# Two chunks' columns by transposing transfers, row factors by element transfers, and a reordered transfer queue in a mixer kernel

## The chip, the cores and the metric

The kernel runs on one core of a Trainium2 chip. The metric is the device time of one execution in microseconds (us), the median of several runs. Engines: PE (TensorE, matrix products and transposes), DVE (VectorE), ACT (ScalarE), POOL (GpSimd), and SP (SyncE), which here only issues transfers.

## The reference

```python
x = A_x                                  # (1, 2048, 512), bf16
xn = _layernorm(x, axis=-1)
s = _A_ref(xn, A_wqkv, A_wo)             # 32 heads of 16, 8 keys at distance 2, softmax, then @ wo
g = _silu(_B_ref(xn, B_w1, B_w2, B_w3, B_w4))
return x + s * g

def _B_ref(x, w1, w2, w3, w4):           # D = 512, F = 1376
    h = _gelu(_layernorm(x, axis=-1) @ w1)
    ...                                  # four groups of columns of h, shifted by 1, 1, 2, 2 rows: g0 to g3
    hs = jnp.concatenate([g0, g1, g2, g3], axis=-1) @ w2
    x1 = x + hs
    return x1 + _gelu(_layernorm(x1, axis=-1) @ w3) @ w4
```

The layer norm in `_B_ref` is applied to rows that are already normalised. It comes down to one more factor per row.

## The kernel before, in words

The 2048 rows are split into even rows (p = 0) and odd rows (p = 1), 1024 each, and each half into two chunks of 512 rows (`CH`): chunks 0 and 1 are even rows, 2 and 3 odd. A chunk is four tiles of 128 rows (`TPC`). `xn[p]` holds rows, with rows on the 128 partitions; `xnT[p]` holds the same numbers with columns on the partitions, which the products need.

For each chunk the front part of the kernel does the following.

- `Norm` (`stats` L221 and L223 on DVE, `root` L204 and L205 on POOL, `apply` L237 on DVE) normalises the rows in place.
- `turn` (L296) gets the columns: each call does eight PE transposes of 128x128 (L302), half a chunk, into a PSUM bank, and one DVE copy (L303) to `xnT`.
- `rows2` (L248) makes the second norm's row factors on POOL: 512 numbers as a 128x4 tile `r2b`.
- The factors have to stand along the free axis, the same on all partitions. `rows2_spread` (L264, chunks 1 and 2) does that by a PE transpose of the 128x4 tile (L266), a DVE copy (L268), a write of four rows of 256 bytes to DRAM (`r2_d`, L269) and a broadcast read of the 1 KB row to 128 partitions (L271). `rows2_here` (L273, chunks 0 and 3) does it on the chip: a diagonal on DVE (L277), one product with ones on PE (L282) and a copy out of PSUM (L284 on ACT, or L286 on DVE).
- `scaled` (L288) multiplies the columns by the factors on DVE (L291) into `xn2Ts[c]`.
- `q_all`, `k_all` and `v_pair` are the projections of mixer A; `w1` (L397) is mixer B's first product with its gelu. `v_pair` also writes its result to DRAM (`v_d`, L377, two transfers of 256 KB a call).

Then `w2` (L415) multiplies the shifted columns of h by w2 and adds the result to the rows; `columns` (L443) normalises, writes the chunk to DRAM (L446) and reads it back with a transposing transfer (L450); `w3` (L459) and the attention with `g_w4` follow.

Every instruction is pinned in program order on its engine, so each engine runs its list from top to bottom and the order in the listing (L501 to L599) is the order on each engine. The same holds for SP: a transfer whose data is not ready holds back all that stand behind it. Transfers use eight semaphores in turn, and a ninth waits for the first. PSUM results go through `pair()`: three pairs of banks in rotation.

The lines around the change: `rows2_spread(1)` at L544, the load of w3 at L545, `turn(2, ..)` at L566 and L567, `turn(3, ..)` at L571 and L572, the load of w4 at L574, `rows2_here(3)` at L579, `w1` of chunks 2 and 3 at L581 to L584, `w2(0)` at L585, `columns(0)` at L586, `w3(0)` at L592.

Of the kernel before, what the change touches and what calls it, by code (L numbers as in the profile page):

```python
# [8 lines left out]
AF = mybir.ActivationFunctionType  # L9
ALU = mybir.AluOpType  # L10
BF16 = mybir.dt.bfloat16
# [9 lines left out]
def kernel(  # L21
# [17 lines left out]
    PE, DVE, ACT, POOL, SP = nc.tensor, nc.vector, nc.scalar, nc.gpsimd, nc.sync  # L39

    def pin(ins):

        return tc.keep_in_program_order(ins)

    P = 128
    S = 2048
    D = 512
    F = 1376
    ND = D // P
# [4 lines left out]
    CH = 512  # L54
    NCH = S // CH
    TPC = CH // P
    M = S // 2
# [21 lines left out]
    dram = ctx.enter_context(tc.tile_pool(name="dram", bufs=1, space=bass.MemoryType.DRAM))  # L79
    psp = ctx.enter_context(tc.tile_pool(name="psp", bufs=1, space=bass.MemoryType.PSUM))  # L80

    def b8(shape, name):
        return big.tile(shape, BF16, name=name, tag="b8")

    def b4(shape, name):
        return sm4.tile(shape, BF16, name=name, tag="b4")
# [9 lines left out]
    def single():  # L96
        cnt["s"] += 1
        return PS[:, 6 + (cnt["s"] - 1) % 2, :]
# [27 lines left out]
    w3_sb = wpl.tile([P, WS], BF16, name="w3_sb", tag="w")[:, 0 : ND * F].rearrange("p (dt f) -> p dt f", f=F)  # L126
# [4 lines left out]
    ident = const.tile([P, P], BF16, name="ident")  # L131
# [61 lines left out]
    xnT = [b8([P, ND, M], f"xnT{p}") for p in range(2)]  # L193
# [2 lines left out]
    kM = [kbp.tile([P, ND, MK, 2], BF16, name=f"kM{p}", tag="kM") for p in range(2)]  # L196
    v_d = [dram.tile([MK, 2, D], BF16, name=f"v_d{p}") for p in range(2)]
    r2_d = dram.tile([NCH, CH], BF16, name="r2_d")
    x1n_dram = dram.tile([S, D], BF16, name="x1n_dram")
    vst = [b4([P, 2, 2, D], f"vst{i}") for i in range(2)]  # L200

# [5 lines left out]
    def small_t(name, shape, dt=F32):  # L207
        return small.tile(shape, dt, name=name, tag=name)
# [33 lines left out]
    def x_of(c):  # L242
        p, k = c // 2, c % 2
        return xn[p][:, k * TPC : (k + 1) * TPC, :]

    xn2Ts, r2s = {}, {}

    def rows2(c, ln):  # L248

        r2 = small_t("r2", [P, TPC])  # L250
        r2b = small_t("r2b", [P, TPC], BF16)
        eng = DVE if c == 0 else POOL
        pin(eng.tensor_tensor(out=r2, in0=ln.rstd, in1=ln.rstd, op=ALU.mult))
        pin(eng.tensor_tensor(out=r2, in0=r2, in1=ln.mv[:, :, 1], op=ALU.mult))
        if c == 0:
            pin(ACT.activation(r2, r2, AF.Sqrt, bias=eps_t[:]))
            with nc.allow_low_precision("bf16 row factors"):
                pin(DVE.reciprocal(out=r2b, in_=r2))
        else:
            rsqrt_eps(r2, r2)  # L260
            pin(POOL.tensor_copy(out=r2b, in_=r2))
        r2s[c] = r2b

    def rows2_spread(c):  # L264
        pt = single().bitcast(BF16)[0:TPC, 0:P]
        pin(PE.transpose(pt, r2s[c], ident[:]))  # L266
        t = small_t("r2t", [TPC, P], BF16)
        pin(DVE.tensor_copy(out=t, in_=pt))  # L268
        pin(SP.dma_start(out=r2_d[c].rearrange("(j q) -> j q", q=P), in_=t))  # L269
        xn2Ts[c] = b4([P, ND, CH], "xn2T")  # L270
        pin(SP.dma_start(out=xn2Ts[c][:, ND - 1, :], in_=r2_d[c : c + 1, :].to_broadcast([P, CH])))  # L271

    def rows2_here(c):  # L273

        xn2Ts[c] = t = b4([P, ND, CH], "xn2T")
        d = t[:, 0, :].rearrange("p (j q) -> p j q", q=P)
        pin(DVE.tensor_tensor(  # L277
            out=d, in0=ident.unsqueeze(1).to_broadcast([P, TPC, P]), in1=r2s[c].unsqueeze(2).to_broadcast([P, TPC, P]),
            op=ALU.mult,
        ))  # L280
        pt = single()
        pin(PE.matmul(pt, lhsT=ones_bf[:], rhs=t[:, 0, :], start=True, stop=True))  # L282
        if c == 0:
            pin(ACT.activation(t[:, ND - 1, :], pt, AF.Copy))  # L284
        else:
            pin(DVE.tensor_copy(out=t[:, ND - 1, :], in_=pt))  # L286

    def scaled(c):  # L288
        p, k = c // 2, c % 2
        t = xn2Ts[c]  # L290
        pin(DVE.tensor_tensor(  # L291
            out=t, in0=xnT[p][:, :, k * CH : (k + 1) * CH],
            in1=t[:, ND - 1, :].unsqueeze(1).to_broadcast([P, ND, CH]), op=ALU.mult,
        ))

    def turn(c, h):  # L296
        p, k = c // 2, c % 2
        i = k * TPC + 2 * h
        pt = single().bitcast(BF16).rearrange("p (a j q) -> p a j q", a=ND, j=2)
        for j in range(2):  # L300
            for dt in range(ND):
                pin(PE.transpose(pt[:, dt, j, :], xn[p][:, i + j, dt * P : (dt + 1) * P], ident[:]))  # L302
        pin(DVE.tensor_copy(  # L303
            out=xnT[p][:, :, i * P : (i + 2) * P], in_=pt.rearrange("p a j q -> p a (j q)")
        ))

    def turn_one(c, t):
        p, k = c // 2, c % 2
        i = k * TPC + t
        pt = single().bitcast(BF16)[:, 0 : ND * P].rearrange("p (a q) -> p a q", a=ND)  # L310
        for dt in range(ND):
            pin(PE.transpose(pt[:, dt, :], xn[p][:, i, dt * P : (dt + 1) * P], ident[:]))
        pin(ACT.activation(xnT[p][:, :, i * P : (i + 1) * P], pt, AF.Copy))

    def q_half(pts, lo, hi, nts=range(ND)):
        for nt in nts:
# [17 lines left out]
    def chunk(t, c):  # L334
        p, k = c // 2, c % 2
        return t[p][:, :, k * CH : (k + 1) * CH]
# [12 lines left out]
    def k_all(c, parts=(0, 1)):  # L349
        p, k = c // 2, c % 2  # L350
        for a in parts:
            pt = proj(c, a, wqk_sb[:, :, D : 2 * D], chunk(xnT, c))
            for e in range(2):
                pin(ACT.activation(  # L354
                    kM[p][:, 2 * a : 2 * a + 2, 8 + k * CH : 8 + (k + 1) * CH, e], pt, AF.Copy, scale=em[:, e : e + 1]
                ))
# [29 lines left out]
    def v_pair(p, t):  # L386
        pt = pair()
        for i in range(2):
            v_mm(p, t + i, pt[:, i, :])
        v_keep(p, t, 2, pt[:, 0, :])  # L390

    def v_pad(p):
        rows = v_d[p].rearrange("r e d -> (r e) d")
        pin(SP.dma_start(out=rows[0:16], in_=zero[0:16, :]))
        pin(SP.dma_start(out=rows[2 * (M + 8) : 2 * MK], in_=zero[0:4, :]))

    def w1(c, a):  # L397
        p, k = c // 2, c % 2
        pt = proj(c, a, w1_sb, xn2Ts[c])
        pin(ACT.activation(  # L400
            hT[p][:, 2 * a : 2 * a + 2, 1 + k * CH : 1 + (k + 1) * CH], pt, AF.Gelu_apprx_tanh
        ))
# [12 lines left out]
    def w2(c, order="a0 s0 a1 s1"):  # L415

        p, k = c // 2, c % 2
        x_c = x_of(c)
        ln = ln2[c] = Norm(x_c, b4([P, TPC, D], "xn3"), TPC, "l3")
        pts = []  # L420
        for h in range(TPC // 2):
            pt = pair()
            pts.append(pt)
            for j in range(2):
                m0 = k * CH + (2 * h + j) * P
                for g in range(ND):
                    pin(PE.matmul(  # L427
                        pt[:, j, :], lhsT=w2_src(p, g, m0), rhs=w2_sb[:, g, :],
                        start=(g == 0), stop=(g == ND - 1),
                    ))  # L430
        for what, i in (w for w in order.split()):
            if what == "a":
                h = int(i)
                xs = x_c[:, 2 * h : 2 * h + 2, :]
                pin(DVE.tensor_tensor(out=xs, in0=pts[h], in1=xs, op=ALU.add))  # L435
            elif what == "s":
                h = int(i)
                ln.stats(2 * h, 2 * h + 2)
            else:
                columns(c - 1)  # L440
        ln.root()
# [87 lines left out]
    for a in range(2):  # L529
# [10 lines left out]
    v_pair(0, 2)  # L540
    k_all(0, (1,))
    v_pad(0)
    w1(0, 0)
    rows2_spread(1)  # L544
    pin(SP.dma_start(out=w3_sb, in_=B_w3.rearrange("(dt q) f -> q dt f", q=P)))  # L545
    turn(1, 0)
    turn(1, 1)
    w1(0, 1)
    l2 = Norm(x_of(2), x_of(2), TPC, "l1")
    l2.stats(0, 4)  # L550
    l2.root()
    l2.apply(0, 4)
    rows2(2, l2)
    l3 = Norm(x_of(3), x_of(3), TPC, "l1")
    l3.stats(0, 4)
    l3.root()
    scaled(1)
    q_all(1)
    k_all(1)
    v_pair(0, 4)  # L560
    l3.apply(0, 4)
    rows2(3, l3)
    v_pair(0, 6)
    rows2_spread(2)
    w1(1, 0)
    turn(2, 0)  # L566
    turn(2, 1)  # L567
    w1(1, 1)
    scaled(2)
    q_all(2)  # L570
    turn(3, 0)  # L571
    turn(3, 1)  # L572
    k_all(2)
    pin(SP.dma_start(  # L574
        out=w4_sb[:, 0 : NF - 1, :],
        in_=B_w4[0 : (NF - 1) * P, :].rearrange("(ft q) n -> q ft n", q=P),
    ))
    pin(SP.dma_start(out=w4_sb[0:FL, NF - 1, :], in_=B_w4[(NF - 1) * P : F, :]))
    rows2_here(3)  # L579
    scaled(3)  # L580
    w1(2, 0)  # L581
    w1(2, 1)
    w1(3, 0)
    w1(3, 1)  # L584
    w2(0)  # L585
    columns(0)  # L586
    v_pad(1)
    q_all(3)
# [289 lines left out]
    for n in range(NU):  # L878
        now["n"] = n
        q = W4 * (n + 1) // NU - given  # L880
# [111 lines left out]
```

## Time and profile before

| what | value |
|---|---|
| time, median of three runs | 197.82 us (197.75 to 199.02) |
| the profiled execution | 197.26 us |
| its span in the trace | 195.5 us, so 1.76 us lie around it |
| granted TensorE clock | 0.996 |
| DVE, ACT, POOL busy | 60%, 68%, 10% of the span |
| transfers | 28.12 MB, mean 144 GB/s |

A time in a list is the start from the beginning of the span and then the duration, both in us; an arrow in brackets names what an engine's idle time ended with. SPq lines are transfers as SP issues them; the duration there is the time of issuing, not of moving the data.

### The profile page before, as it was taken

How to read it: one execution, taken by the hardware profiler on the slowest of the kernel's cores; microseconds unless marked ns; L12 is line 12 of the kernel's file. 1: busy time of each engine (PE TensorE's matmuls, PEld its weight loads, DVE VectorE, ACT ScalarE, POOL GpSimd, SP SyncE). 2: the span in 40 equal slices, each digit the busy share in tenths (PEclk: the TensorE clock that was granted, in tenths of full speed). 3: DMA queues.
4: the chain of work that ended last, by engine and by line, in shares of the span. 5: the costliest groups of instructions: out<-in, count | busy, mean ns of one | idle time of the engine just before them, and what ended most of it. 6: DMA issues, size and time to landing. Idle time of an engine off the chain costs nothing.

```text
span 195.5 us, 5255 instructions
## 1 busy us (share of the span) xinstructions
PE 185.5 (95%) x2253; PEld 91.8 (47%) x2283; DVE 117.8 (60%) x229; ACT 133.3 (68%) x151; POOL 19.1 (10%) x57
## 2 busy tenths in 40 slices
PE   7899999999999999999999999999999999999990
PEld 2474544554444444444444444445444544554540
DVE  5785767236076697494200035556487888798894
ACT  7399769649817615435656588877887876887871
POOL 3006066100002022006000000000000000000000
PEclk9999999999999999999999999999999999999998
DMA  4997480654000433752480051457565556582523
GB/s 131 339 368 239 132 282 15 218 158 157 0 0 3 136 83 109 215 107 65 110 260 0 0 162 60 157 166 232 153 216 161 137 155 215 127 247 51 171 91 126
DMA packets 33576, 28.12 MB, mean 144 GB/s; under 512 B 10760, under 2 KB 32528, under 8 KB 33552
## 3 DMA queue, kind: packets, MB, share of 16 engines
q1 hardware_dynamic: 33408, 27.71, 47.2%
q8 instruction: 18, 0.29, 0.6%
q10 hardware_dynamic: 144, 0.07, 0.1%
q14 instruction: 6, 0.05, 0.1%
HBM read 17.01 MB, written 8.67 MB: 131 GB/s over the span
## 4 chain that ended last, share of the span: by engine, by line
PE 85%; DMA 5%; DVE 4%; issue 2%; SPq 1%; ACT 1%
PE PS L469 19%; PE PS L328 19%; PE PS L764 19%; PE PS L427 5%; PE PS L811 4%; PE PS L795 4%; PE PS L652 3%; DMA wqk_sb<-in_A_wqkv_dram 3%; PE PS L626 3%; PE PS L362 3%; DMA x1nT<-x1n_dram 2%; PE PS L318 2%; PE PS L662 2%; PE PS L302 2%; DVE sg L825 2%
## 5 line engine op out<-in xcount | busy, mean ns | idle before, releaser
L469 PE MATMUL PS<-x1nT,w_sb 128*128 128x512 bf16 (+1 forms) x173 | 38.2, 379 | 0.4 <-DMA x1nT<-x1n_dram 0.3
L633 ACT ACTIVATE prob<-PS 128x1824 bf16<-128x1824 f32 x18 | 30.4, 1688 | 4.4 <-PE PS L626 3.6
L764 PE MATMUL PS<-w_sb,h3a 128*128 128x512 bf16 x112 | 29.2, 379 | 1.9 <-issue 1.7
L475 ACT ACTIVATE h3a<-PS 128x1024 bf16<-128x1024 f32 x16 | 16.4, 1024 | 21.0 <-PE PS L469 19.1
L777 DVE TENSOR_TENSOR xn<-PS,xn 128x512 bf16<-128x512 f32 x15 | 10.3, 686 | 32.0 <-PE PS L764 31.8
L469 PEld LDWEIGHTS <-w_sb 128*128 128x128 bf16 (+1 forms) x176 | 17.5, 100 | 20.9 <-issue 0.7
L328 PE MATMUL PS<-xnT,wqk_sb 128*128 128x512 bf16 x109 | 25.0, 379 | 0.2
L354 ACT ACTIVATE kM<-PS,em 128x1024 bf16<-128x1024 f32 x16 | 20.8, 1404 | 3.2 <-PE PS L328 3.2
L638 DVE TENSOR_TENSOR prob<-prob,maskb 128x1824 bf16<-128x1824 bf16 x18 | 19.8, 1102 | 1.8 <-ACT prob L633 1.8
L764 PEld LDWEIGHTS <-h3a 128*128 128x128 bf16 x128 | 11.3, 97 | 13.4 <-issue 1.2
L328 PEld LDWEIGHTS <-wqk_sb 128*128 128x128 bf16 x112 | 10.9, 98 | 12.8
L435 DVE TENSOR_TENSOR xn<-PS,xn 128x1024 bf16<-128x1024 f32 x8 | 9.6, 1213 | 11.3 <-PE PS L427 11.3
L811 PE MATMUL PS<-wo_sb,oT 128*128 128x512 bf16 (+1 forms) x68 | 15.5, 366 | 0.0
L328 PE MATMUL PS<-xn2T,w_sb 128*128 128x512 bf16 x62 | 14.6, 379 | 0.1
L427 PE MATMUL PS<-w_sb,hT 128*128 128x512 bf16 x63 | 14.4, 379 | 0.1
L821 ACT ACTIVATE sg<-PS 128x512 bf16<-128x512 f32 (+1 forms) x17 | 9.6, 572 | 6.1 <-PE PS L811 6.1
L764 PE MATMUL PS<-w_sb,h3b 128*128 128x512 bf16 (+1 forms) x44 | 12.8, 380 | 0.8 <-issue 0.8
L339 ACT ACTIVATE qT<-PS 128x1024 bf16<-128x1024 f32 x8 | 8.1, 1024 | 7.6 <-PE PS L328 7.6
L373 ACT ACTIVATE vst<-PS 128x512 bf16<-128x512 f32 (+1 forms) x12 | 8.8, 743 | 3.5 <-ACT sig L784 2.3
L221 DVE BATCH_NORM_STATS2 l1s<-xn 128x6 f32<-128x512 bf16 x16 | 10.1, 680 | 1.6 <-DMA xn<-in_A_x_dram 1.6
L400 ACT ACTIVATE hT<-PS 128x1024 bf16<-128x1024 f32 x8 | 8.1, 1031 | 3.8 <-PE PS L328 3.8
L221 DVE BATCH_NORM_STATS2 l3s<-xn 128x6 f32<-128x512 bf16 x16 | 10.2, 682 | 0.2
(105 smaller groups left out, 229.2 us busy)
## 6 DMA issues: line engine op xcount, KB each, us to landing
ring<-v_d SPq DMA_DIRECT2D x18, 256.0 KB, 3.3
v_d<-vst SPq DMA_DIRECT2D x16, 256.0 KB, 2.7
x1n_dram<-xn SPq DMA_DIRECT2D x4, 512.0 KB
xo<-in_A_x_dram SPq DMA_DIRECT2D x8, 256.0 KB, 4.1
ring<-rec_d SPq DMA_DIRECT2D x4, 456.0 KB, 4.7
out_dram<-xo SPq DMA_DIRECT2D x7, 256.0 KB
xn<-in_A_x_dram SPq DMA_DIRECT2D x6, 256.0 KB, 7.9
w_sb<-in_B_w_dram SPq DMA_DIRECT2D x1, 1376.0 KB
```

The source lines that it names most:

```text
L221: pin(DVE.bn_stats(out=self.st[:, j, :], in_=self.src[:, j, :]))
L328: pin(PE.matmul(pt[:, b, :], lhsT=w[:, dt, nt * P : (nt + 1) * P], rhs=rhs[:, dt, :], start=(dt == 0), stop=(dt == ND - 1),))
L354: pin(ACT.activation(kM[p][:, 2 * a : 2 * a + 2, 8 + k * CH : 8 + (k + 1) * CH, e], pt, AF.Copy, scale=em[:, e : e + 1]))
L427: pin(PE.matmul(pt[:, j, :], lhsT=w2_src(p, g, m0), rhs=w2_sb[:, g, :], start=(g == 0), stop=(g == ND - 1),))
L435: pin(DVE.tensor_tensor(out=xs, in0=pts[h], in1=xs, op=ALU.add))
L469: pin(PE.matmul(pt[:fs, ft % 2, :], lhsT=w3_sb[:, dt, ft * P : ft * P + fs], rhs=x1nT[:, dt, :], start=(dt == 0), stop=(dt == ND - 1),))
L475: pin(ACT.activation(t[:, o : o + 2, :], pt, AF.Gelu_apprx_tanh))
L633: pin(ACT.activation(pr, S_ps[:, :, 0 : ND * NQ], AF.Exp, scale=SCALE))
L638: pin(DVE.tensor_tensor(out=f, in0=f, in1=maskb[:], op=ALU.min))
L764: pin(PE.matmul(pt, lhsT=h3_of(c, ft)[:fs, jj * P : (jj + 1) * P], rhs=w4_sb[:fs, ft, :], start=(ft == 0), stop=(ft == NF - 1 and silu < 2),))
L777: pin(DVE.tensor_tensor(out=x_i, in0=pt, in1=x_i, op=ALU.add))
L811: pin(PE.matmul(pt[:, 0:W], lhsT=oT[p][:, dt, i * P : (i + 1) * P], rhs=wo["sb"][:, dt, c], start=(dt == 0), stop=(dt == ND - 1),))
```

## The change

The listing's order changes, and two helpers are new. Chunks 2 and 3 get their columns by a write of the normalised rows to a DRAM buffer and a transposing read, instead of PE transposes. The row factors of chunks 1, 2 and 3 go to DRAM straight from the 128x4 tile, with one element of two bytes per descriptor, and are read back by the same broadcast as before; the write and the read are separate calls now. `w2(0)` stands ahead of `w1(3, 1)`. The loads of w3 and w4 stand further back in SP's queue.

```diff
+    xn_d = {1: dram.tile([M, D], BF16, name="xn_d")}
...
-    def rows2_spread(c):
-        pt = single().bitcast(BF16)[0:TPC, 0:P]
-        pin(PE.transpose(pt, r2s[c], ident[:]))
-        t = small_t("r2t", [TPC, P], BF16)
-        pin(DVE.tensor_copy(out=t, in_=pt))
-        pin(SP.dma_start(out=r2_d[c].rearrange("(j q) -> j q", q=P), in_=t))
+    def rows2_write(c):
+        pin(SP.dma_start(out=r2_d[c].rearrange("(j q) -> q j", q=P), in_=r2s[c]))
+
+    def rows2_read(c):
         xn2Ts[c] = b4([P, ND, CH], "xn2T")
         pin(SP.dma_start(out=xn2Ts[c][:, ND - 1, :], in_=r2_d[c : c + 1, :].to_broadcast([P, CH])))
...
+    def turn_dma(c):
+        p, k = c // 2, c % 2
+        pin(SP.dma_start(
+            out=xn_d[p].rearrange("(i q) d -> q i d", q=P)[:, k * TPC : (k + 1) * TPC, :], in_=x_of(c)
+        ))
+        pin(SP.dma_start_transpose(out=xnT[p][:, :, k * CH : (k + 1) * CH], in_=xn_d[p][k * CH : (k + 1) * CH, :]))
...
     v_pad(0)
+    rows2_write(1)
     w1(0, 0)
-    rows2_spread(1)
-    pin(SP.dma_start(out=w3_sb, in_=B_w3.rearrange("(dt q) f -> q dt f", q=P)))
     turn(1, 0)
     turn(1, 1)
+    rows2_read(1)
     w1(0, 1)
...
     l2.apply(0, 4)
+    turn_dma(2)
     rows2(2, l2)
+    rows2_write(2)
...
     scaled(1)
     q_all(1)
     k_all(1)
+    l3.apply(0, 4)
+    turn_dma(3)
+    rows2_read(2)
+    rows2(3, l3)
+    rows2_write(3)
     v_pair(0, 4)
-    l3.apply(0, 4)
-    rows2(3, l3)
     v_pair(0, 6)
-    rows2_spread(2)
+    rows2_read(3)
+    pin(SP.dma_start(out=w3_sb, in_=B_w3.rearrange("(dt q) f -> q dt f", q=P)))
     w1(1, 0)
-    turn(2, 0)
-    turn(2, 1)
     w1(1, 1)
     scaled(2)
     q_all(2)
-    turn(3, 0)
-    turn(3, 1)
     k_all(2)
+    scaled(3)
     pin(SP.dma_start(
         out=w4_sb[:, 0 : NF - 1, :],
...
-    rows2_here(3)
-    scaled(3)
     w1(2, 0)
     w1(2, 1)
     w1(3, 0)
+    w2(0)
     w1(3, 1)
-    w2(0)
     columns(0)
```

More of the change, by code (lines that the diff above doesn't have):

```diff
@@ L282, in rows2_here @@
         pin(PE.matmul(pt, lhsT=ones_bf[:], rhs=t[:, 0, :], start=True, stop=True))
[L283 to L286, printed above, removed]
+        pin(ACT.activation(t[:, ND - 1, :], pt, AF.Copy))
     def scaled(c):
```

## The prediction

> **What bounds the kernel now.** I read the page's busy table first, then the chain of work that ended last, then SP's and DVE's timelines from 18 to 72 us, where the change lies, and last the transfers' rates in a few short windows.
>
> ```profile
> PE 185.5 (95%) x2253; PEld 91.8 (47%) x2283; DVE 117.8 (60%) x229; ACT 133.3 (68%) x151; POOL 19.1 (10%) x57
> ```
>
> PE is busy 95% of the span, so what counts is PE work removed and PE waits added. The chain, for 18 to 75 us:
>
> ```profile
> 20.25 0.15 PE PS L266
> ...
> 33.48 0.15 PE PS L266
> 33.63 1.83 PE PS L328 x8
> 35.46 0.89 PE PS L302 x16
> 36.36 4.53 PE PS L328 x21
> ...
> 41.54 0.89 PE PS L302 x16
> 42.43 3.45 PE PS L328 x16
> 45.88 0.22 PE PS L282
> 46.10 3.02 PE PS L328 x14
> ...
> 66.16 4.51 DMA x1nT<-x1n_dram
> ```
>
> PE has no hole here: the transposes (L302), the row transposes (L266) and the product with ones (L282) are themselves on the chain. Only the last line is no PE work: w3(0) starts at 70.80 after 0.27 us of waiting for its transposed columns. SP and DVE:
>
> ```profile
> 34.40 2.52 SPq L377 DMA_DIRECT2D v_d<-vst  x4
> 37.01 0.47 SPq L269 DMA_DIRECT2D r_d<-r2t  x1
> 39.26 0.34 SPq L271 DMA_DIRECT2D xn2T<-r_d  x1
> ...
> 63.17 0.39 SPq L446 DMA_DIRECT2D x1n_dram<-xn  x1
> 66.16 2.20 SPq L450 DMA_TRANSPOSE x1nT<-x1n_dram  x1
> ```
>
> ```profile
> 42.37 1.23 DVE L291 TENSOR_TENSOR xn2T<-xnT,xn2T 128x2048 bf16<-128x2048 bf16 x1 [5.13 <-DMA xn2T<-r_d]
> ```
>
> The same transfers that the change adds stand here: a 512 KB write takes 2.99 us until the transfer that reads it is issued, a transposing read 2.20 us of SP's issuing and 4.51 us to its user, a broadcast read 3.11 us (39.26 to 42.37). DVE sat 5.13 us idle for row factors, harmlessly, since w1(2) came only at 46.10.
>
> **What is removed.** From PE: two row transposes (2 x 0.15), the 32 transposes of chunks 2 and 3 (2 x 0.89), one product with ones (0.22): 2.30 us, all on the chain. Putting w2(0) ahead of w1(3,1) gives the chain from w2(0) over DRAM to w3(0) 1.73 us (eight products) more cover, so the 0.27 us wait goes too. The gain is 2.57 us if nothing new waits. The DVE work removed (two row copies of 0.20, four column copies of 0.65, a diagonal of 0.68, a cast of 0.69) is not on the path; nor is ACT, with one near miss: w1(3,0) needs the bank pair that ACT empties 6.94 us after k_all(2) starts, and PE would now be there after 6.90, which I leave out at 0.05. The loads of w3 and w4 now start near 45 us: 2.75 MB at the 360 GB/s of the plain transfers end near 55, w3 is used at 70 and w4 after 112, and the next write to DRAM comes near 60, so I cost the move at nothing; were w3 late, w3(0) would pay for it in full.
>
> **What is added, in time order.** All of it goes through SP's one queue, and the data runs in the order of issue:
>
> ```profile
> DMA packets 2176, 0.94 MB, mean 303 GB/s; under 512 B 1664, under 2 KB 2176, under 8 KB 2176
> ...
> x1n_dram<-xn SPq DMA_DIRECT2D x1, 512.0 KB
> ```
>
> That is the window from 79.9 to 83.0 us: a write issued at 79.93, two us behind a transposing read. The 256-byte packets of the read fill the engines until 81.3, and only then do the write's 1 KB packets come; its next step came 3.44 us after issue instead of 2.99. So I add up times on the data queue. A transposing read's packets end 3.7 us after its issue (66.16, last near 69.9), a 512 KB write holds the queue 1.6 us (64.1 to 65.7) and counts as landed 0.55 later, a broadcast read has its 128 packets at some 90 GB/s, 1.5 us, and its user starts 0.4 later. The four v_d writes take 3.1 us of the queue at the 340 GB/s they ran at.
>
> The unknown is the element write: 512 packets of two bytes into one KB; no row shows one. Lower bound: 32 packets on each of 16 engines at the 18 ns of the transposing read's 256-byte packets, 0.6 us. Upper: the broadcast read, whose 128 packets all read one KB, moves a packet in 1.5 / 128 = 11.7 ns over all engines; 512 such take 6 us. Nearest are the 228-byte packets of the reciprocals' write near 135.5 us, also small packets to DRAM, 120 in a quarter of a us at their densest: 512 take 1.07 us, which I take.
>
> Chunk 1: the element write goes out at 21.15, behind the v_d pads, its read near 23.3, done near 26; scaled(1) comes at 30.2. Four us of cover, no cost.
>
> Chunk 2's columns: apply ends at 27.64 (27.79 before, less one row transpose), the write is issued at 27.67, the transposing read at 30.66, done at 35.17. q_all(2) is due at 37.92 - 1.19 = 36.73. Covered by 1.5 us.
>
> Then it gets tight. The read's packets end at 34.36, the element write of chunk 2 behind them at 35.43, chunk 3's write (issued at 34.07 after apply) at 37.03, landed 37.58. SP stands at the transposing read of chunk 3 until then, and behind it wait both remaining broadcast reads, an element write, the four v_d writes, w3 and w4. It is issued from 37.58 to 39.78, its packets end at 41.28. The broadcast read of chunk 2 follows: 42.78, usable at 43.2; scaled(2) (1.23 on DVE) ends at 44.43. w1(2,0) was due at 46.10 - 2.30 = 43.80: a wait of 0.7 us. Chunk 3's element write ends at 43.85 and lands at 44.4, and SP issues the broadcast read only then; the v_d writes are ahead of it in the queue until 46.95. I give the read 0.8 us beyond that (engines that are done early start early), 0.4 to its user, 1.3 for scaled(3) with its hand-over: 49.45. w1(3,0) was due at 47.25, and behind it on PE stand w2(0) and everything else. The wait is 2.20 us in all, the first 0.7 included.
>
> Sum: -2.57 + 2.20 = -0.37 us. The profiled execution would take 196.9, and the median, 0.56 higher, 197.4.
>
> The own range: with 0.6 us for the element writes and a broadcast read of 1.2 then 0.5, the same steps give a wait of 0.6, net -2.0; with 1.6 and 1.5, 3.95, net +1.4: 195.8 to 199.2.
>
> [...] In the trace the transposing read's packets take 2.4 us for 512 KB (67.5 to 69.9) and the plain write's 1.6. [...]
>
> **The rivals.**
>
> *Element writes are slow, and the kernel gets slower.* Each us more of an element write is paid twice: chunk 2's stands ahead of chunk 3's columns, chunk 3's ahead of v_d and the last broadcast read. The sum is zero at 1.25 us and +1% at 2.25; with 3 us it is -0.37 + 2 x 1.93 = +3.5, so 201.3; with 6 us, +9.5. For it: 512 writes into one KB, and the broadcast read, also on one KB, runs at 90 GB/s where plain transfers run at 360. Against it: the 228-byte packets ran at 18 to 22 ns each. [...]
>
> *The queue does not hold back what is small.* If the broadcast reads land 3.11 us after issue, as at 39.26, whatever is ahead of them, w1(3,0) waits 0.4 us and the sum is -2.2: 195.6. Against it: the window above.
>
> *Chunk 2's columns are late at q_all(2).* If the write took the 3.85 us of the slowest such row (91.02 to 94.87), they would be there at 36.0, still in time; beyond 36.73 PE waits. What makes them late moves the rest of the queue too, so I price 1.5 us beyond it at +1.1: 198.9. Little speaks for it; the queue is empty then.
>
> **The numbers.** [...] A measurement here can tell about 1% (2 us) from no change. Forecast, late columns and that rate lie within it, 0.61, of which I move 0.03 to slower for the forecast's upper end: faster 0.12, same 0.58, slower 0.30. The range goes from 195.6, the best rival, to 201.4, just past an element write of 3 us; what is slower still, some 0.13, is left out.
>
> **What would show it.** L302 with 24 instead of 56 transposes, no L266, PE at q_all(2) near 36.7 without a wait. Then a PE wait ahead of w1(2,0) of some 0.7 us and one ahead of w1(3,0) of some 1.5, both ended by DVE's multiplication, that one by the broadcast read; SP standing before the second transposing read until some 37.6. w3(0) starting without a wait near 70.2. The prediction is wrong if the element write's packets take much more or less than 1.07 us, or if the broadcast reads overtake.

## The result, and the profile after

The changed kernel takes 244.38 us (median of four runs, 242.64 to 245.49) against 197.78 us before: a ratio of 1.2365, 95% interval 1.232 to 1.241. The forecast was 197.4 us, with 201.4 as the upper end. Some executions of a kernel come out over 1.5% above its fastest, and the ratios in this document leave those out (four of the eight of the first experiment). The profiled execution took 244.97 us, its span is 243.3 us, 47.8 us more than before.

The page, its first, second and fourth part (PEclk is the granted TensorE clock in tenths, one digit per fortieth of the span):

```profile
span 243.3 us, 5192 instructions
...
PE 190.6 (78%) x2218; PEld 91.3 (38%) x2248; DVE 113.8 (47%) x221; ACT 133.6 (55%) x151; POOL 18.2 (7%) x57
...
PEclk9999995879869555899999999999999999999998
...
PE 55%; DMA 29%; ACT 4%; SPq 4%; DVE 4%; issue 2%
```

PE has 35 instructions fewer, but is busy 5 us longer, because its clock is down for part of the first half (granted clock 0.920 over the span, 0.996 before). DMA, 5% of the chain before, is 29% of it.

PE's timeline from 40 to 127 us, where each line is a run of products and the bracket is the wait ahead of it:

```profile
41.19 4.99 PE L331 MATMUL PS<-xn2T,w_sb 128*128 128x512 bf16 x16 [7.93 <-DVE xn2T L287]
50.56 8.55 PE L331 MATMUL PS<-xnT,wqk_sb 128*128 128x512 bf16 x31 [4.37 <-DMA xnT<-xn_d]
68.11 5.18 PE L331 MATMUL PS<-xn2T,w_sb 128*128 128x512 bf16 x16 [9.01 <-DVE xn2T L287]
94.24 3.60 PE L331 MATMUL PS<-xn2T,w_sb 128*128 128x512 bf16 x8 [20.95 <-DVE xn2T L287]
97.63 4.10 PE L430 MATMUL PS<-w_sb,hT 128*128 128x512 bf16 x16
...
117.34 9.66 PE L472 MATMUL PS<-x1nT,w_sb 128*128 128x512 bf16 x43
```

In order: w1 of chunk 1, q_all(2) with k_all(2), w1 of chunk 2, w1(3,0), w2(0) and w3(0); w1(3,0) is the first half of w1 of chunk 3. The four waits are 42.3 us. The runs behind them are slow as well: 16 products took 4.99 and 5.18 us where the same 16 took 3.62 before, 8 took 3.60 in place of 1.89, q_all(2) and k_all(2) 8.55 in place of 7.07, w2(0) 4.10 in place of 3.62. That is 6.6 us. Near the first products behind each wait the granted clock was 0.50 (42 to 44, 51 to 54, 68 to 70 and 94 to 97 us). 42.3 + 6.6 less the 2.57 us that the change removes is 46.3; w3(0) starts 46.54 us later than before (117.34 against 70.80). The other 1.3 us of the span come behind w3(0), most of them in two gaps of PE of 0.6 us after 190 us.

Three of the waits end with scaled on DVE (L287), and that waits for row factors, as its line in the page's fifth part says (four instructions, 59.0 us of idle time ahead of them):

```profile
L287 DVE TENSOR_TENSOR xn2T<-xnT,xn2T 128x2048 bf16<-128x2048 bf16 x4 | 4.9, 1218 | 59.0 <-DMA xn2T<-r_d 59.0
```

SP's timeline shows why they are late. L266 is the element write, L270 the broadcast read, L313 and L316 the write and the transposing read of the columns:

```profile
21.89 0.39 SPq L266 DMA_DIRECT2D r_d<-r2b  x1
35.56 0.34 SPq L270 DMA_DIRECT2D xn2T<-r_d  x1
36.00 0.39 SPq L313 DMA_DIRECT2D xn_d<-xn  x1
41.36 1.92 SPq L316 DMA_TRANSPOSE xnT<-xn_d  x1
43.38 0.52 SPq L266 DMA_DIRECT2D r_d<-r2b  x1
43.99 0.46 SPq L313 DMA_DIRECT2D xn_d<-xn  x1
61.31 2.08 SPq L316 DMA_TRANSPOSE xnT<-xn_d  x1
63.48 0.54 SPq L270 DMA_DIRECT2D xn2T<-r_d  x1
64.08 0.42 SPq L266 DMA_DIRECT2D r_d<-r2b  x1
64.58 2.56 SPq L380 DMA_DIRECT2D v_d<-vst  x4
87.48 0.34 SPq L270 DMA_DIRECT2D xn2T<-r_d  x1
```

Chunk 1's element write lands 13.67 us after its issue (21.89 to 35.56, the read that waits for it), for 1 KB. SP stands at that read meanwhile, so chunk 2's columns go out only at 36.00, and q_all(2) waits for them. Behind chunk 2's element write, the plain 512 KB write at 43.99 lands after 17.3 us instead of the 2.99 of before. Chunk 3's element write, with the v_d writes behind it, lands after 23.4 (64.08 to 87.48). What the transfer engines did in the 13 us from 22.6 to 35.6 us (their busy share in forty slices, then the packets):

```profile
DMA  2500000000400000000000000000000000000000
...
DMA packets 529, 0.01 MB, mean 1 GB/s; under 512 B 528, under 2 KB 528, under 8 KB 528
```

The 512 packets of two bytes went through in the first two slices, 0.65 us; then nothing moved for 12 us but one load of instructions, and the transfer still had not landed. So the time lies behind the packets, as the trace records them, and not in them.

### The profile page after: what moved, and what is told of

Its sections match the earlier page's. It is cut to its first block, busy times and chain, and to the rows that moved or that the text cites. A ratio compares the mean times of both kernels' runs of the same rounds, so it can differ in the third digit from the quotient of the medians.

```text
span 243.3 us, 5192 instructions
## 1 busy us (share of the span) xinstructions
PE 190.6 (78%) x2218; PEld 91.3 (38%) x2248; DVE 113.8 (47%) x221; ACT 133.6 (55%) x151; POOL 18.2 (7%) x57
## 4 chain that ended last, share of the span: by engine, by line
PE 55%; DMA 29%; ACT 4%; SPq 4%; DVE 4%; issue 2%
PE PS L472 16%; PE PS L768 15%; DMA r_d<-r2b 15%; DMA xn_d<-xn 9%; PE PS L331 5%; PE PS L430 4%; ACT kM L357 3%; PE PS L815 3%; PE PS L799 3%; PE PS L656 2%; PE PS L630 2%; DMA wqk_sb<-in_A_wqkv_dram 2%; DMA xn2T<-r_d 2%; PE PS L666 2%; SPq L316 2%
## 5 line engine op out<-in xcount | busy, mean ns | idle before, releaser
L331 PE MATMUL PS<-xn2T,w_sb 128*128 128x512 bf16 x63 | 19.4, 467 | 37.9 <-DVE xn2T L287 37.9
L287 DVE TENSOR_TENSOR xn2T<-xnT,xn2T 128x2048 bf16<-128x2048 bf16 x4 | 4.9, 1218 | 59.0 <-DMA xn2T<-r_d 59.0
L331 PE MATMUL PS<-xnT,wqk_sb 128*128 128x512 bf16 x109 | 26.4, 398 | 4.5 <-DMA xnT<-xn_d 4.4
L331 PEld LDWEIGHTS <-w_sb 128*128 128x128 bf16 x64 | 7.0, 114 | 48.9 <-DVE xn2T L287 39.1
L430 PE MATMUL PS<-w_sb,hT 128*128 128x512 bf16 x63 | 14.9, 388 | 0.1
L342 ACT ACTIVATE qT<-PS 128x1024 bf16<-128x1024 f32 x8 | 8.1, 1024 | 10.4 <-PE PS L331 10.4
```

The source lines that it names most:

```text
L331: pin(PE.matmul(pt[:, b, :], lhsT=w[:, dt, nt * P : (nt + 1) * P], rhs=rhs[:, dt, :], start=(dt == 0), stop=(dt == ND - 1),))
L430: pin(PE.matmul(pt[:, j, :], lhsT=w2_src(p, g, m0), rhs=w2_sb[:, g, :], start=(g == 0), stop=(g == ND - 1),))
```

## The experiments

Theory M was that the element writes are the whole loss. Rival T was that the columns by transposing transfers, or SP standing for them, cost the time.

**The changed kernel with row factors as rows.** The tile is turned on PE and copied on DVE as before, and four rows of 256 bytes are written; SP's order and the transposing transfers stay. The turns stand where POOL's factors are there, and the v_d writes are held back to keep SP's order; w1(1,0) stands sooner for that.

```diff
+    def rows2_turn(c):
+        pt = single().bitcast(BF16)[0:TPC, 0:P]
+        pin(PE.transpose(pt, r2s[c], ident[:]))
+        r2ts[c] = t = small_t("r2t", [TPC, P], BF16)
+        pin(DVE.tensor_copy(out=t, in_=pt))
...
-        pin(SP.dma_start(out=r2_d[c].rearrange("(j q) -> q j", q=P), in_=r2s[c]))
+        pin(SP.dma_start(out=r2_d[c].rearrange("(j q) -> j q", q=P), in_=r2ts[c]))
...
```

> The changed kernel, but the row factors of chunks 1, 2 and 3 are turned by a PE transpose and a DVE copy as before and go to DRAM as four rows of 256 bytes; the order of SP's transfers is that of the changed kernel, and the transposing transfers stay. Theory M (the element writes: 512 writes of two bytes into one KB keep the memory busy some 12 us after their packets have left the queue, and hold back what is behind them): nearly all of the 47 us go, 195.5 to 198.5 us, my working of the prediction with 0.1 us for the row write gives -2.57 + 0.45 + 0.5 = 196.2. Rival T (the transposing reads, or SP waiting for the writes ahead of them, cost the time): over 210 us, the waits ahead of q_all(2) and w1(2,0) stay at 4 and 9 us.

Measured: 199.82 us, the median of eight runs from 197.42 to 202.38; the ratio to before 1.0029 (0.9989 to 1.0068). Nearly all 47 us go with the two-byte writes: theory M, and rival T falls. But 196.2 was too low. PE's timeline, w1(2) and w1(3,0), is from an execution of 201.94 us, in which the first w1 starts at 21.61 us instead of 18.36. PE and SP are shifted alike from there (3.36 us at w1 of chunk 1, 3.35 at chunk 2's write, against the kernel with factors made on the chip below), so I read the waits as they stand:

```profile
48.00 3.63 PE L339 MATMUL PS<-xn2T,w_sb 128*128 128x512 bf16 x16 [0.40 <-DVE xn2T L295]
53.49 1.90 PE L339 MATMUL PS<-xn2T,w_sb 128*128 128x512 bf16 x8 [1.87 <-DVE xn2T L295]
```

The broadcast reads behind the transposing read and the v_d writes still make PE wait 2.27 us, not 0.5. They reached DVE 4.16 us and 5.05 us after their issue (42.55 to 46.71 and 47.16 to 52.21), against 3.11 before. With 0.45 us of row transposes put back, -2.57 + 0.45 + 2.27 = +0.15. Even with rows in place of elements, the change as it stands is worth nothing.

**The kernel before with element writes for chunks 1 and 2.**

```diff
-        pt = single().bitcast(BF16)[0:TPC, 0:P]
-        pin(PE.transpose(pt, r2s[c], ident[:]))
-        t = small_t("r2t", [TPC, P], BF16)
-        pin(DVE.tensor_copy(out=t, in_=pt))
-        pin(SP.dma_start(out=r2_d[c].rearrange("(j q) -> j q", q=P), in_=t))
+        pin(SP.dma_start(out=r2_d[c].rearrange("(j q) -> q j", q=P), in_=r2s[c]))
```

> The kernel before, with element writes for the row factors of chunks 1 and 2 in place of the PE transpose and the copy, nothing else moved. Theory M: chunk 1's write lands some 13.7 us after 21.2, so scaled(1) ends near 39 and w1(1,0) waits some 6 us; chunk 2's write stands behind w3 and the v_d writes and lands 15 to 25 us after its issue, so w1(2,0) waits 10 us or more; with the slower clock after the waits 215 to 230 us in all. Rival T: within 2 us of before.

Measured: 222.98 us in one run. PE's timeline:

```profile
42.34 3.59 PE L324 MATMUL PS<-xn2T,w_sb 128*128 128x512 bf16 x8 [9.15 <-DVE xn2T L287]
...
69.56 0.58 PE L278 MATMUL PS<-xn2T,ones_bf 128*128 128x512 bf16 x1 [12.64 <-DVE xn2T L273]
```

Two element writes and no transposing transfer of columns beside them cost 25 us. Rival T would have had none of it. The writes landed as expected (13.68 us for chunk 1's, 20.43 for chunk 2's), but the first wait is 9.15 us and not 6: the broadcast read behind chunk 1's write took 6.0 us to its user (35.06 to 41.06), with the load of w3 right behind it.

**The factors of chunks 2 and 3 made on the chip.** `rows2_here` on DVE and PE in place of write and read; chunk 1 by turned rows; columns, w2(0), w3 and w4 as in the changed kernel.

```diff
...
-    rows2_write(2)
...
-    rows2_read(2)
...
-    rows2_write(3)
...
-    rows2_read(3)
...
+    rows2_here(2)
     w1(1, 1)
     scaled(2)
     q_all(2)
+    rows2_here(3)
     k_all(2)
...
```

> The changed kernel with the row factors of chunks 2 and 3 made on the chip (diagonal on DVE, a product with ones on PE, a copy on DVE) and of chunk 1 by turned rows as before, so that no row factor stands in SP's queue beside the transposing transfers. Theory M: no PE wait between 15 and 70 us; PE work falls by 1.78 - 0.07 us and the 0.27 us wait goes, -2.0 us in all: 195.8 us. Rival T: over 205 us.

Measured: 197.35 us (median of ten), ratio 0.9968 (0.9938 to 0.9998). The same kernel once more, in more executions:

> The kernel of the run e5_here once more in five rounds, to tell 1% from nothing: by its trace PE reaches w3(0) 1.92 us sooner than before, so 195.9 us, a ratio of 0.990; if the sooner work is lost again later, 0.997 as in the three rounds.

Measured: 197.64 us (median of twelve), ratio 0.9973 (0.9941 to 1.0005). It is a gain of some 0.3%, at the edge of what can be told, not the 1% expected. PE in the first of the two:

```profile
44.24 5.58 PE L338 MATMUL PS<-xn2T,w_sb 128*128 128x512 bf16 x24
...
68.88 9.66 PE L479 MATMUL PS<-x1nT,w_sb 128*128 128x512 bf16 x44
...
157.80 0.23 PE L671 MATMUL PS<-prob,den_st 128*32 128x114 bf16 x3 [0.87 <-issue]
```

No wait stands before w1(2) or w3(0), which starts 1.92 us sooner than before (2.33 in the second profiled execution). Of that, 0.09 and 0.54 us lie ahead of the change (the first w1 starts at 18.27 and 17.82 instead of 18.36), so the change brings 1.8 us up to w3(0). So the columns by transposing transfers do what they were to do. The gain is lost in part between 140 and 165 us, where PE stops in the middle of a run, with nothing waited for that the trace shows: once for 0.87 us here, for 0.88 and 0.60 in the second. The profiled execution of before has none, but the same code with lone writes at its end (below) has one of 0.65 and one of 0.95 us at 159 us in its two executions, so such gaps do not come with the change alone. From w3(0) to PE's last run it is 114.0, 114.5 and 114.8 us in these three and 114.8 and 116.3 here. Why the gaps come was not settled, and with them it stays open how much of the 1.8 us is kept.

**Lone writes at the end of the kernel before.** Each write goes to a buffer of its own, and a small read waits for it, in essence:

```python
pin(SP.dma_start(out=d.rearrange("(j q) -> q j", q=P), in_=r))   # d: 512 elements; r: 128x4
pin(SP.dma_start(out=back, in_=d))                               # its issue shows when d has landed
```

> The kernel before, and behind its last store a row of lone transfers on SP, each a write to a DRAM buffer of its own and a small read that waits for it, so that the time from the write's issue to the read's issue is its landing. Control of 4 rows of 256 bytes: 1.3 to 2.3 us. 512 elements of two bytes into one KB: 13.7 us, as in the changed kernel; half as many: 7.5. The same 512 elements 64 bytes and 512 bytes apart: about 2.5 to 4 us each if what costs is many writes into the same small piece of memory, 13 us again if any write of two bytes costs it. 128 writes of eight bytes into one KB: 4.4 us if the count of writes into one KB decides. 512 writes of 64 bytes, end to end: 3 us if same pieces matter, 13 us if every write below 512 bytes costs it. A plain 512 KB write alone: 3.0 us; the same right behind an element write: 14 to 17 us by theory M, some 4 if the element write holds nothing back.

SP's timeline; a write's landing is the start of the read below it less its own start:

```profile
195.39 0.39 SPq L967 DMA_DIRECT2D p_elem<-r2b  x1
209.40 0.21 SPq L969 DMA_DIRECT2D back<-p_elem  x1
209.66 0.39 SPq L967 DMA_DIRECT2D p_half<-r2b  x1
224.60 0.21 SPq L969 DMA_DIRECT2D back<-p_half  x1
224.86 0.38 SPq L967 DMA_DIRECT2D p_far<-r2b  x1
226.95 0.21 SPq L969 DMA_DIRECT2D back<-p_far  x1
...
235.45 0.38 SPq L985 DMA_DIRECT2D p_big<-xn  x1
238.43 0.21 SPq L986 DMA_DIRECT2D back<-p_big  x1
238.69 0.38 SPq L990 DMA_DIRECT2D p_elem<-r2b  x1
239.12 0.50 SPq L985 DMA_DIRECT2D p_big<-xn  x1
255.35 0.24 SPq L986 DMA_DIRECT2D back<-p_big  x1
```

The element write takes 14.0 us alone. Half as many, into 512 bytes, take 14.9, which I had expected to halve. The same 512 elements 64 bytes apart take 2.09 us, 512 bytes apart 1.82; 128 runs of eight bytes 2.87, 512 of 64 bytes end to end 2.73, four rows of 256 bytes 1.31. So neither the number of writes nor their being small costs the time by itself, but how small and how close together they are. The last four lines show the holding back: a 512 KB write lands after 2.98 us alone and after 16.2 right behind an element write.

**Spacings, and two queues.** The same arrangement.

> The kernel before, and behind its last store lone writes to DRAM as in the run probe. 512 elements of two bytes, 4, 8, 16 and 32 bytes apart. Theory L: the landing grows with the number of writes in one piece of 64 bytes (16, 8, 4, 2): about 8, 5, 3.5 and 2.6 us; if the piece is 32 bytes, the last is 2.1. Rival P (the count of writes to the whole transfer's region matters): all near 14 or falling with the region only slightly. 512 elements without gaps: 14 again. 256 writes of four bytes into one KB: 8 us by L (16 writes in 64 bytes). 128 of eight: 2.9 again. 1024 elements of two bytes into two KB: 14 by L (as many in each 64 bytes, the pieces side by side), 28 if the writes of a transfer go one by one. Last, an element write on ACT's queue at the same time as a plain 512 KB write on SP's: the plain one lands after 3 to 4 us if only the own queue is held back, after 12 us or more if the transfer engines or the memory are.

| write | writes per 64 bytes | landing, us |
|---|---|---|
| 512 x 2 bytes, end to end | 32 | 13.6 |
| 1024 x 2 bytes, end to end | 32 | 13.8 |
| 512 x 2 bytes, 4 bytes apart | 16 | 10.9 |
| 256 x 4 bytes, end to end | 16 | 9.5 |
| 512 x 2 bytes, 8 bytes apart | 8 | 4.1 |
| 128 x 8 bytes, end to end | 8 | 2.75 |
| 512 x 2 bytes, 16 bytes apart | 4 | 2.6 |
| 512 x 2 bytes, 32 bytes apart | 2 | 2.0 |

Theory L has the order right and the sizes off (10.9, 4.1 and 2.6 us for its 8, 5 and 3.5). Twice as many elements over twice the place take the same time, and half as many over half the place no less (14.9), so over this span the total count does not matter. A fixed price per write does not fit the rows: over 2.0 us, the first row is (13.6 - 2.0) / 31, or 0.37 us, for each further write in 64 bytes, 256 x 4 bytes 0.50, 512 x 2 bytes 8 bytes apart 0.30, 128 x 8 bytes 0.11. Whether 64 bytes are the right piece to count by stays open, as 32 bytes apart costs no more than 64 (2.0 and 2.09 us). What changes along the rows is also how many partitions write into one piece; no run separates that from the number of writes. (The write 4 bytes apart ran beside the kernel's last stores.) On two queues, with the element write on ACT's, issued at 256.89, and on SP's only a write of eight-byte runs ahead of the plain one:

```profile
257.26 0.44 SPq L988 DMA_DIRECT2D s_big<-xn  x1
274.15 0.23 SPq L989 DMA_DIRECT2D back<-s_big  x1
```

The plain write on SP's queue lands after 16.9 us all the same (behind eight-byte runs alone, in the next run, it was 4.9). So being on the same queue is not what holds it; what does was not shown.

**The changed kernel with runs of eight bytes.** The four factors of a partition stand side by side, 128 writes; the broadcast read goes to a tile of its own (`fr`), and `scaled` reads it permuted.

```diff
-        pin(SP.dma_start(out=r2_d[c].rearrange("(j q) -> q j", q=P), in_=r2s[c]))
+        pin(SP.dma_start(out=r2_d[c].rearrange("(q j) -> q j", q=P), in_=r2s[c]))
...
+                in1=fr[c].rearrange("p (q j) -> p j q", j=TPC).unsqueeze(1).to_broadcast([P, ND, TPC, P]), op=ALU.mult,
...
```

> The changed kernel with one thing altered: the 128x4 tile goes to DRAM as 128 runs of eight bytes (a row's four factors side by side) in place of 512 of two bytes, and scaled reads the broadcast factors in permuted order. No PE transpose, the same order on SP. Theory L (what costs is that many writes of two bytes fall into the same 64 bytes): the lone landing of 2.9 us holds, the transfers behind are not held for long, PE waits 3 to 5 us in all ahead of w1(2,0) and w1(3,0), because the permuted read also makes each DVE multiplication slower, by 1 us or so: 197 to 201 us. Rival S (a write from a 128x4 tile to DRAM is slow in this place whatever its runs): over 235 us.

Measured: 207.72 us, ratio 1.0514 (1.0463 to 1.0565). Neither number: 37 us of the 47 go with the shape of the write, although the permuted reading costs some again; rival S excludes that, but it is 7 us above theory L's upper end. PE:

```profile
48.56 6.04 PE L339 MATMUL PS<-xn2T,w_sb 128*128 128x512 bf16 x16 [4.59 <-DVE xn2T L289]
57.21 3.41 PE L339 MATMUL PS<-xn2T,w_sb 128*128 128x512 bf16 x8 [2.61 <-DVE xn2T L289]
```

The waits are 7.2 us, and the products behind them take 6.04 and 3.41 us for 3.62 and 1.89: another 3.9 us, which the expectation left out. Chunk 3's 512 KB write, behind the eight-byte writes, landed after 4.9 us instead of 3.0, and the permuted multiplication took 2.25 to 2.29 us instead of 1.23.

**w2(0) back behind w1(3,1)**, otherwise the kernel with factors made on the chip.

```diff
     w1(3, 0)
-    w2(0)
     w1(3, 1)
+    w2(0)
```

> The run e5_here with w2(0) behind w1(3,1) again, as in the kernel before. If putting w2(0) sooner is what removed the wait ahead of w3(0), the wait comes back, at 0.3 us or somewhat more, as PE reaches w3(0) 1.7 us sooner while the chain over DRAM from w2(0) to it is as long as before; nothing else changes. If other things made it go, no wait.

Measured: 197.36 us in one run. The w2 run ahead of w3(0), and w3(0):

```profile
61.68 7.31 PE L437 MATMUL PS<-w_sb,hT 128*128 128x512 bf16 x32
69.16 9.66 PE L479 MATMUL PS<-x1nT,w_sb 128*128 128x512 bf16 x44 [0.17 <-DVE l3m L224]
```

The bracket names DVE's L224, but with w2(0) sooner w3(0) starts at 68.88 while the same instruction has only begun (68.87 to 69.17), so PE does not need it. The transposing read fits: it is issued at 64.64, 4.52 us ahead of w3(0), and 4.64 us ahead in the kernel before. From the start of the w2 run to w3(0) it is 7.48 us here, 7.57 in the kernel before and 7.13 to 7.16 in the five traces with w2(0) sooner: some 0.35 us come back. The move is right, and too small to be told from the time of one execution.

## Why the prediction was wrong

- **What is removed** was right. PE does 24 transposes of columns and no row transposes, w3(0) starts without a wait, and with the factors of chunks 2 and 3 made on the chip the change brings 1.8 us up to w3(0), where 1.78 - 0.07 + 0.27 says 1.98.
- **The element write** is the step that failed. I took 1.07 us from the 228-byte packets and 6 us as the upper bound from the broadcast read. Through the queue it was no slower than my lower bound (0.6 us), and it landed 13.7 us after issue. Both bounds priced packets on the queue. The rows I took them from say nothing of many writes into one small piece; nor does any row of before. The unknown was named, and its bound was not one.
- **Chunk 1, "four us of cover, no cost"**, failed for that reason: 7.93 us of wait.
- **Chunk 2's columns** were late, by 4.37 us, but not by the rival's way (a slow write of the columns). Their write was issued at 36.00 and not at 27.67, because SP stood behind chunk 1's element write. With the factors made on the chip the write went out at 27.72 and the read at 30.70, as worked out (27.67 and 30.66), and nothing waited.
- **The two-fold price** ("each us more is paid twice") was right in direction and too low: it would give about +24 us for 12 us more. Chunk 1's wait, the slow products and the v_d writes caught up with chunk 3's (23.4 us) were not in it.
- **The rival of slow element writes** named the right transfer, the right place (many writes into one KB) and the right side, with 0.27 against 0.56 for the forecast. It still priced time on the queue, and its highest price, +9.5, was a fifth of what came. No change had 0.58, and all that is slower than 201.4 some 0.13.
- **The order of the queue** was right: with row writes, at hardly any cost on the queue, the reads behind the transposing read and the v_d writes made PE wait 2.27 us, against my 2.20 with the element writes' 1.07 in it. That the two waits agree is luck: the same steps with 0.1 us for the write gave 0.5, so this term was too small as well, by some 1.8 us. The rival that nothing small is held back falls with the same run (4.16 and 5.05 us for the broadcast reads, not 3.11).
- **The clock** was missing. I treated a wait as costing its own length. Four waits of 4.4 us and more cost 6.6 us on top, as the products behind them ran slowly, at a granted clock of 0.50 near their starts.
- One small slip changed nothing: a forecast of -0.37 us puts w3(0) at 70.4 and not near 70.2.

## What to carry to other kernels

A transfer's packets and its landing are two prices: here a write of 512 single elements into neighbouring addresses had its packets through in 0.65 us, landed some 14 us after its issue, and held back a plain 512 KB write to 16.2 us on the same queue and 16.9 on another, against 2.98 alone. Write such numbers in longer runs, by turning the tile on the chip first; one PE transpose of 0.15 us was the cheap way here, and four rows of 256 bytes landed in 1.31 us. When a cost has no row in the trace, do not take the queue's packet rate for its bound: price also that its user waits far longer than the packets take, and put the slow products behind a long PE wait into the sum (6.6 us behind four waits here).

## What the runs showed of the hardware that was not expected

- Writes of two bytes to DRAM: 2.0 us to land at 32 bytes apart, 13.6 to 14.9 us end to end, the same for 256, 512 and 1024 of them within 10% (one execution each, two for 512).
- While they are outstanding, plain writes crawl: a 512 KB write took 16.2 us on the same queue and 16.9 on another, against 2.98 alone.
- Behind a wait of PE the products can run at half the clock. In the changed kernel the granted clock fell to 0.50 some 5 us into the wait of 20.95 us and stayed there from 79 to 98 us; around the wait of 4.37 us it was 0.50 from 51 to 54. In the run with eight-byte runs it was 0.50 from 57.2 to 58.8 us and 0.55 on average from 58.8 to 60.5, behind a wait of 2.61 us; it had been 0.50 from 48.5 to 53 us as well, behind the wait of 4.59 us, and 0.88 and 0.93 on average from 53 to 55 and from 55 to 57.2. Around a wait of 1.87 us in the run with row writes it stayed at 1.00 (51.6 to 55.2 us).
